# Another order of the three part products of every split float32 product, by tile, row pair and pass

## The chip, the cores and the metric

The kernel runs on one core of a Trainium2 chip. The metric is device time in microseconds (us) for one execution: 725.29 us before the change, the median of three runs from 724.9 to 725.68.

## The reference, cut to what matters

```python
g = sigmoid((x * gate_w).sum(-1, keepdims=True))          # x: 2048 x 576
q, k, v = split(x @ wqkv)                                 # 32 heads of 18
pq, pk = phi(q), phi(k)                                   # phi(t) = t+1 for t>0, else exp(t); + 1e-6
kv = einsum("bhsd,bhse->bhde", pk, v); z = pk.sum(s)      # linear attention
a = ((pq @ kv) / (pq . z + 1e-6)) @ wo
b = Cr @ (x @ Wr.T) - Ci @ (x @ Wi.T)                     # real part of a 2-D DFT; C: 2048 x 2048, W: 576 x 576
out = g * a + (1 - g) * b
```

## The kernel before, in words

TensorE multiplies here with operands rounded to a short float32 format. So each operand is held as two tiles, a high part (`hi_of`, an ACT copy into the short format, line 175) and a low part (`lo_of`, what is left over, a DVE subtraction, line 185), and each product of float32 matrices is made of **three part products** that add up in one PSUM bank: high by high (hh), high by low (hl) and low by high (lh). The first letter is the stationary operand, the second the moving one. A group of three is called a triple here. In `hh hl` and `hl hh` the two neighbours have the same stationary operand, in `hh lh` and `lh hh` the same moving one. Nearly all matmuls have a moving operand of 128 x 288 and a stationary one of 128 x 128.

The stages, in order of time, with the lines of their matmuls in the profile:

1. K (L532 for the first four row tiles, then L205, operands `wd` and `xs`): x times wk, 12 tiles of 28 matmuls, `steps` gives the order hh hl lh for each of four chunks of 128, and two matmuls for the rest.
2. x transposed times the features of k (L696, `pk` and `c`): per quarter four row tiles, three part products, two column halves that alternate (two banks); the order is `FULL`, hh hl lh. The small products with wv (L678, L681) follow.
3. Q (L205, `wd` and `xs`): as K, 16 tiles.
4. The attention output (L205, `mw` and `qs`): `m_steps`, 16 tiles, hh hl lh, `qs` being the transposed and normalised q. `transposed` makes the two `qs` tiles of a pair: TensorE transposes (L797), ACT makes the high parts, DVE the low parts. The low part is the last thing that a tile's first triple needs.
5. The hidden DFT (L979, `Hidden.product`): a 2x2 scheme with seven products in place of eight; for each of eight row tiles p seven products of two triples in the order `TURN` = hl hh lh and one matmul of 96 rows for the rest.
6. The sequence DFT (L1133, `sequence`): again seven products (the dictionary `PRODUCTS`, run in the order 1, 6, 2, 5, 7, 3, 4), eight row pairs j, each in four batches b of two inner tiles: a batch is 7 products x 2 tiles x 3 = 42 matmuls. Seven of the eight PSUM banks hold the seven sums of a row pair. Order `TURN`, and `FULL` in the very first batch. Behind the fourth batch of a row pair ACT and DVE read the banks in the order 1, 6 and 2, 7, 5, 7, 3, 4, combine them and store two row tiles.

Stages 5 and 6 run twice, for the real and the imaginary matrices. ACT and DVE make the high and low parts of the next batch of the matrix (`craw` to `c`) while TensorE multiplies. ACT, DVE and SP run in the order in which the code is written; TensorE does so from stage 4 on, and in stages 1 to 3 a scheduler sets its order.

Of the kernel before, what the change touches and what calls it, by code (L numbers as in the profile page):

```python
# [133 lines left out]
def kernel(  # L134
# [67 lines left out]
    def run(ps, pairs):  # L202
        pairs = list(pairs)
        for n, (a, b) in enumerate(pairs):
            nc.tensor.matmul(ps, a, b, start=(n == 0), stop=(n == len(pairs) - 1))  # L205

    def half(h):
        return slice(h * HALF, (h + 1) * HALF)
# [62 lines left out]

    def steps(xs, rhs):

        for c in range(KC):
            yield xs[:, c], rhs(c)
            yield xs[:, c], rhs(5 + c)
            yield xs[:, 5 + c], rhs(c)
        yield xs[:, 4], rhs(4)
        yield xs[:, 9], rhs(4)
# [407 lines left out]
    for c in range(5):  # L687
        ps = [bank(), bank()]
        passes = FULL if c < KC else FULL[:2]
        for q in range(NCU):  # L690
            t = xg_split.pop(0)
            for k in range(CU):
                s = q * CU + k
                for n, (a, b) in enumerate(passes):
                    for h in range(2):
                        nc.tensor.matmul(ps[h][:, :HALF], t[:, a, k], pk[s][:, b, half(h)],  # L696
                                         start=(s == 0 and n == 0),
                                         stop=(s == NT - 1 and n == len(passes) - 1))
            tick()
# [47 lines left out]
    def q_tile(i):  # L747
        xs = kept.pop(0) if i < KEPT else split.pop(0)
        for h in range(2):
            ps = bank()[:, :QH[h]]  # L750
            run(ps, steps(xs, lambda j: wqt.row(h, j)))
# [111 lines left out]

    def m_steps(qs, h):
        for c in range(KC):
            yield qs[:, c], mhi[:, c, half(h)]
            yield qs[:, c], mlo[:, c, half(h)]
            yield qs[:, 4 + c], mhi[:, c, half(h)]
        yield qs[:, 8], mhi[:, KC, half(h)]
        yield qs[:, 8], mlast[:, half(h)]  # L870
# [68 lines left out]
    class Hidden:  # L939
# [34 lines left out]
        def product(self, ps, p, k, start):  # L974
            x, (w, wl) = self.x[p, k], self.w[k]
            ops = [(x[:, a, c * P:c * P + P], w[:, 2 * c + b]) for c in range(2) for a, b in TURN]
            ops.append((self.rest[p][:96, 6 - k], wl[:96]))
# [113 lines left out]
    mix_ring = Ring(MIX_AT, D * 4, 4)  # L1091

    def sequence(m, g, src, dst, last=None, between=None):
        late, held, stores, rest_lows = [], [], [], []
        for n in range(NP * NB):
# [30 lines left out]
            if end and b == NB - 2:  # L1126
                continue
            for q, (l, f) in PRODUCTS.items():
                for b, c in held:
                    for k in range(BS):  # L1130
                        p = b * BS + k
                        for i, (x, y) in enumerate(TURN if n or b else FULL):
                            nc.tensor.matmul(ps[q], c[x][:, l, k], factors[p](y, f),  # L1133
                                             start=(p == 0 and i == 0),
                                             stop=(p == NP - 1 and i == 2))
            held.clear()
# [56 lines left out]
    for i in range(NT):  # L1193
# [162 lines left out]
```

## Time and profile before

| what | value |
|---|---|
| median of three runs | 725.29 us |
| the profiled execution's own time | 725.31 us |
| its span | 723.6 us |
| outside the span | 1.71 us |
| granted TensorE clock | 1.00 |
| matmuls and weight loads | 5436 each |
| of them L1133 / L205 / L979 / L696 | 2688 / 1266 / 784 / 448 |

PE in the profile's lines is the matmul, PEld the weight load that precedes each. A matmul's record lasts about 294 ns, though a new one begins every 132 ns, because records overlap in the pipeline. So the pace of a stage is read as the time from the first to the last start, divided by the number of matmuls less one, and not from the mean duration.

### The profile page before, as it was taken

How to read it: one execution, taken by the hardware profiler on the slowest of the kernel's cores; microseconds unless marked ns; L12 is line 12 of the kernel's file. 1: busy time of each engine (PE TensorE's matmuls, PEld its weight loads, DVE VectorE, ACT ScalarE, POOL GpSimd, SP SyncE). 2: the span in 40 equal slices, each digit the busy share in tenths (PEclk: the TensorE clock that was granted, in tenths of full speed). 3: DMA queues.
4: the chain of work that ended last, by engine and by line, in shares of the span. 5: the costliest groups of instructions: out<-in, count | busy, mean ns of one | idle time of the engine just before them, and what ended most of it. 6: DMA issues, size and time to landing. Idle time of an engine off the chain costs nothing.

```text
span 723.6 us, 13786 instructions
## 1 busy us (share of the span) xinstructions
PE 718.9 (99%) x5436; PEld 718.3 (99%) x5436; DVE 594.6 (82%) x954; ACT 331.8 (46%) x519; POOL 54.1 (7%) x94
## 2 busy tenths in 40 slices
PE   9999999999999999999999999999999999999998
PEld 9999999999999999999999999999999999999997
DVE  5699876787999828989999999857889988778884
ACT  5998445678644534453434334223535432342331
POOL 1112200050131100000010000000000000000000
PEclk9999999999999999999999999999999999999999
DMA  7388887874594699544475586889963543454440
GB/s 256 105 286 297 305 304 214 295 223 118 182 358 177 228 321 388 160 153 131 157 249 189 167 289 198 287 313 401 380 214 130 175 143 136 125 179 153 153 154 34
DMA packets 54836, 157.83 MB, mean 218 GB/s; under 512 B 6388, under 2 KB 12084, under 8 KB 53748
## 3 DMA queue, kind: packets, MB, share of 16 engines
q1 hardware_dynamic: 45716, 118.44, 48.5%
q0 software_dynamic: 8768, 38.12, 14.5%
q8 instruction: 43, 0.70, 0.4%
q10 hardware_dynamic: 288, 0.39, 0.2%
q14 instruction: 21, 0.17, 0.1%
HBM read 114.06 MB, written 41.39 MB: 215 GB/s over the span
## 4 chain that ended last, share of the span: by engine, by line
PE 93%; DVE 6%; issue 0%; ACT 0%; DVEq 0%; POOL 0%; POOLq 0%
PE bank L1133 49%; PE bank L205 18%; PE bank L979 14%; PE bank L696 8%; PE bank L532 2%; DVE qs L185 1%; DVE acc L775 1%; DVE pz L767 1%; DVE den L768 1%; PE bank L231 1%; PE bank L678 0%; DVE xb L185 0%; DVE den L772 0%; PE bank L797 0%; DVE xb L195 0%
## 5 line engine op out<-in xcount | busy, mean ns | idle before, releaser
L1133 PE MATMUL bank<-fh,c 128*128 128x288 f32 x1792 | 354.7, 294 | 0.0
L1133 PEld LDWEIGHTS bank<-fh,c 128*128 128x128 f32 x1792 | 286.7, 188 | 0.0
L1133 PE MATMUL bank<-fl,c 128*128 128x288 f32 x896 | 263.6, 294 | 0.0
L175 ACT ACTIVATE c<-craw 128x1792 fp32r<-128x1792 f32 (+1 forms) x84 | 121.3, 1447 | 169.9 <-DVE craw L195 161.2
L1133 PEld LDWEIGHTS bank<-fl,c 128*128 128x128 f32 x896 | 168.7, 188 | 0.0
L185 DVE TENSOR_TENSOR c<-craw,c 128x1792 fp32r<-128x1792 f32 (+4 forms) x86 | 141.9, 1653 | 1.5 <-ACT c L175 1.4
L195 DVE TENSOR_TENSOR craw<-craw 128x256 f32<-128x256 f32 (+1 forms) x192 | 97.9, 512 | 22.0 <-DMA craw<-in_ci_dram 13.6
L205 PE MATMUL bank<-wd,xs 128*128 128x288 f32 (+1 forms) x784 | 105.9, 295 | 0.0
L205 PEld LDWEIGHTS bank<-wd,xs 128*128 128x128 f32 x784 | 104.6, 188 | 0.0
L979 PE MATMUL bank<-wf,xf 128*128 128x288 f32 x588 | 91.1, 295 | 0.0
L979 PEld LDWEIGHTS bank<-wf,xf 128*128 128x128 f32 x588 | 83.4, 189 | 0.0
L205 PE MATMUL bank<-mw,qs 128*128 128x288 f32 x448 | 61.8, 296 | 0.1
L696 PE MATMUL bank<-pk,c 128*128 128x288 f32 x448 | 60.6, 296 | 0.0
L205 PEld LDWEIGHTS bank<-mw,qs 128*128 128x128 f32 x448 | 59.8, 188 | 0.5 <-DVE qs L185 0.4
L696 PEld LDWEIGHTS bank<-pk,c 128*128 128x128 f32 x448 | 59.7, 189 | 0.0
L370 DVE SCALAR_TENSOR_TENSOR acc<-bank,e 128x288 f32<-128x288 f32 x64 | 28.5, 452 | 17.3 <-ACT e L369 17.1
L195 DVE TENSOR_TENSOR ys<-bank,ys 128x288 f32<-128x288 f32 x63 | 28.8, 456 | 16.0 <-PE bank L1133 12.6
L185 DVE TENSOR_TENSOR fl<-fl,fh 128x864 fp32r<-128x864 f32 (+1 forms) x32 | 34.5, 1093 | 6.6 <-ACT fh L175 5.3
L175 ACT ACTIVATE fh<-fl 128x864 fp32r<-128x864 f32 (+1 forms) x32 | 29.8, 950 | 16.6 <-DVE fl L195 16.6
L195 DVE TENSOR_TENSOR fl<-bank,y 128x288 f32<-128x288 f32 x48 | 21.6, 450 | 15.8 <-PE bank L979 15.8
L979 PE MATMUL bank<-wf,xr 96*128 96x288 f32 x112 | 33.3, 298 | 0.0
L195 DVE TENSOR_TENSOR ys<-ys,bank 128x288 f32<-128x288 f32 x47 | 21.2, 450 | 12.4 <-PE bank L1133 11.8
(106 smaller groups left out, 639.6 us busy)
## 6 DMA issues: line engine op xcount, KB each, us to landing
xf<-xm SPq DMA_DIRECT2D x42, 512.0 KB, 8.4
craw<-in_cr_dram SPq DMA_DIRECT2D x32, 512.0 KB, 3.6
craw<-in_ci_dram SPq DMA_DIRECT2D x32, 512.0 KB, 3.7
xm<-xb POOLq DMA_DIRECT2D x8, 1024.0 KB, 5.8
wf<-wm SPq DMA_DIRECT2D x14, 576.0 KB, 6.2
xraw<-in_xa_dram SPq DMA_DIRECT2D x25, 320.0 KB, 3.5
xr<-xr SPq DMA_DIRECT2D x14, 448.0 KB, 8.0
xm<-xb POOLq DMA_DIRECT2D x8, 768.0 KB, 7.4
```

What stands on the lines that cost most here:

```text
L175: return nc.scalar.activation(dst, src, AF.Copy, bias=bias)
L185: nc.vector.tensor_tensor(out=dst, in0=src, in1=hi, op=ALU.subtract)
L195: nc.vector.tensor_tensor(out=dst, in0=a, in1=b, op=op)
L205: nc.tensor.matmul(ps, a, b, start=(n == 0), stop=(n == len(pairs) - 1))
L231: nc.tensor.matmul(warm[:, :P], ones_f, ones_f, start=True, stop=True)
L370: nc.vector.scalar_tensor_tensor(dst, ps, 0.0, e, op0=ALU.max, op1=ALU.add)
L532: nc.tensor.matmul(ps[i][h], x[:, i_x * P:(i_x + 1) * P], wkt.row(h, j), start=(c == 0 and n == 0), stop=(c == KC and n == 1))
L696: nc.tensor.matmul(ps[h][:, :HALF], t[:, a, k], pk[s][:, b, half(h)], start=(s == 0 and n == 0), stop=(s == NT - 1 and n == len(passes) - 1))
L767: nc.vector.scalar_tensor_tensor(pz, acc[2 * k + i], EPS, zb, op0=ALU.add, op1=ALU.mult)
L768: nc.vector.tensor_reduce(out=d[:, i], in_=pz.rearrange("p (h d) -> p h d", d=DH), op=ALU.add, axis=AX.X)
L979: nc.tensor.matmul(ps, a, b, start=(start and n == 0), stop=(n == len(ops) - 1), skip_group_check=True)
L1133: nc.tensor.matmul(ps[q], c[x][:, l, k], factors[p](y, f), start=(p == 0 and i == 0), stop=(p == NP - 1 and i == 2))
```

## The change

The order inside the triples, and in places the order of halves, inner tiles and products, now varies:

- `TURNS` lists the six orders of a triple: 0 `hl hh lh`, 1 `lh hh hl`, 2 `hh hl lh`, 3 `hh lh hl`, 4 `lh hl hh`, 5 `hl lh hh`. K, Q and the attention output take order i % 6 for row tile i, the hidden DFT p % 6 for row tile p, stage 2 the order (4c + q) % 6 for chunk c and quarter q; in six of its quarters all of the first half come ahead of the second.
- The sequence DFT keeps its order in the first batch of a sequence and in the last batch of each row pair. In the other batches the first sequence takes order j % 6 for row pairs 0 to 5 and mixtures of orders 0 and 1 for 6 and 7; the second takes order 0 or 1 or both by product, with the inner tiles interleaved for j = 0, the products in the order 1, 2, 6, 5, 3, 7, 4 for j = 1 and 2, and in reversed order for j = 5 and 6.

No matmul is added or taken away, and none has other operands.

```diff
+    TURNS = "hl hh lh", "lh hh hl", "hh hl lh", "hh lh hl", "lh hl hh", "hl lh hh"
+    def orders(turn):
+        return [tuple("hl".index(c) for c in part) for part in turn.split()]
...
-    def steps(xs, rhs):
+    def steps(xs, rhs, turn="hh hl lh"):
         for c in range(KC):
-            yield xs[:, c], rhs(c)
-            yield xs[:, c], rhs(5 + c)
-            yield xs[:, 5 + c], rhs(c)
+            for a, b in orders(turn):
+                yield xs[:, 5 * a + c], rhs(5 * b + c)
...
-        run(ps, steps(xs, lambda j: wkt.row(h, j)))
+        run(ps, steps(xs, lambda j: wkt.row(h, j), TURNS[i % 6]))
...
-            for k in range(CU):
-                s = q * CU + k
-                for n, (a, b) in enumerate(passes):
-                    for h in range(2):
+            turn = passes if c == KC else orders(TURNS[(c * NCU + q) % 6])
+            parts = [(k, n, h) for k in range(CU) for n in range(len(turn)) for h in range(2)]
+            if 6 <= c * NCU + q < 12:
+                parts.sort(key=lambda part: part[2])
+            for k, n, h in parts:
...
-        ops = [... for c in range(2) for a, b in TURN]
+        ops = [... for c in range(2) for a, b in orders(TURNS[p % 6])]
...
+    def variant(j, second):
+        A, B = (orders(turn) for turn in TURNS[:2])
+        first, by = list(PRODUCTS), False
+        mixed = 1, 2, 6, 5, 3, 7, 4
+        if not second:
+            t = orders(TURNS[j % 6])
+            turned = ([t, t], [t, t]) if j < 6 else ([(A, B), (B, A)][j - 6],) * 2
+        else:
+            turned = [[t, t] for t in ((A, A), (A, A), (B, B), (B, A), (A, B), (A, A), (B, B),
+                                       (A, A))[j]]
+            by = j == 0
+            if j in (1, 2):
+                first = mixed
+            if j in (5, 6):
+                first = first[::-1]
+        return first, turned, by
...
-            for q, (l, f) in PRODUCTS.items():
+            turned = [TURN, TURN], [TURN, TURN]
+            first, by = list(PRODUCTS), False
+            if n == 0:
+                turned = [FULL, FULL], [FULL, FULL]
+            elif b < NB - 1:
+                first, turned, by = variant(j, last is not None)
+            for q in first:
+                l, f = PRODUCTS[q]
                 for b, c in held:
-                    for k in range(BS):
-                        p = b * BS + k
-                        for i, (x, y) in enumerate(TURN if n or b else FULL):
+                    parts = [(k, i) for k in range(BS) for i in range(3)]
+                    if by:
+                        parts.sort(key=lambda part: part[1])
+                    for k, i in parts:
+                        p, (x, y) = b * BS + k, turned[f % 2][k][i]
...
-            run(ps[:, :HALF], m_steps(qs, h))
+            run(ps[:, :HALF], m_steps(qs, h, TURNS[i % 6]))
```

`m_steps` is changed as `steps` is, and the Q tiles take the order i % 6 as the K tiles do.

**Place 1**: TensorE in the attention output, the first half of row tile i = 10 (order 4 now). `mw_222` is the high and `mw_223` the low part of the matrix, `qs_364` holds both parts of q; the rows are in the program's order, a wait stands at the matmul that it holds up. Before:

```order
L205 MATMUL bank_3196<-mw_222_1735,qs_364_3128 128x288 [waits Activation_49]
L205 MATMUL bank_3196<-mw_223_1736,qs_364_3128 128x288
L205 MATMUL bank_3196<-mw_222_1735,qs_364_3128 128x288 [waits DVE_49]
L205 MATMUL bank_3196<-mw_222_1735,qs_364_3128 128x288
L205 MATMUL bank_3196<-mw_223_1736,qs_364_3128 128x288
```

With the change:

```order
L205 MATMUL bank_3196<-mw_222_1735,qs_364_3128 128x288 [waits DVE_49]
L205 MATMUL bank_3196<-mw_223_1736,qs_364_3128 128x288 [waits Activation_49]
L205 MATMUL bank_3196<-mw_222_1735,qs_364_3128 128x288 x2
L205 MATMUL bank_3196<-mw_223_1736,qs_364_3128 128x288
L205 MATMUL bank_3196<-mw_222_1735,qs_364_3128 128x288 x2
```

The matmul that waits for DVE's low part has moved from the third place to the first, ahead of the two that need the high part alone.

**Place 2**: TensorE in the first sequence DFT, row pair j = 1, first batch (order 1 now). `c_507` is the high and `c_508` the low part of the matrix (stationary), `fh` and `fl` those of the factor (moving). Before:

```order
L1133 MATMUL bank_4389<-fl_414_3508,c_507_4279 128x288 [waits Activation_49]
L1133 MATMUL bank_4389<-fh_412_3506,c_507_4279 128x288
L1133 MATMUL bank_4389<-fh_412_3506,c_508_4280 128x288 [waits DMAHW6_49,DVE_49]
L1133 MATMUL bank_4389<-fl_423_3584,c_507_4279 128x288
L1133 MATMUL bank_4389<-fh_421_3582,c_507_4279 128x288
L1133 MATMUL bank_4389<-fh_421_3582,c_508_4280 128x288
```

With the change:

```order
L1164 MATMUL bank_4389<-fh_412_3506,c_508_4280 128x288 [waits DMAHW6_49,DVE_49]
L1164 MATMUL bank_4389<-fh_412_3506,c_507_4279 128x288 [waits Activation_49]
L1164 MATMUL bank_4389<-fl_414_3508,c_507_4279 128x288
L1164 MATMUL bank_4389<-fh_421_3582,c_508_4280 128x288
L1164 MATMUL bank_4389<-fh_421_3582,c_507_4279 128x288
L1164 MATMUL bank_4389<-fl_423_3584,c_507_4279 128x288
```

The triple runs backwards: the low part of the matrix is wanted two matmuls earlier, and neighbours still share one operand.

**Place 3**: TensorE in the second sequence DFT, row pair j = 5, first batch, from its first matmul on (products reversed now). `bank_7871` is the sum of product 1, `bank_7872` of product 6, `bank_7876` of product 3 and `bank_7877` of product 4; these names are the program's, which physical bank stands behind one is settled when it is first written. Before:

```order
L1133 MATMUL bank_7871<-fl_656_6083,c_807_7760 128x288 [waits Activation_49]
L1133 MATMUL bank_7871<-fh_654_6081,c_807_7760 128x288
L1133 MATMUL bank_7871<-fh_654_6081,c_808_7761 128x288 [waits DMAHW2_49,DVE_49]
L1133 MATMUL bank_7871<-fl_665_6159,c_807_7760 128x288
L1133 MATMUL bank_7871<-fh_663_6157,c_807_7760 128x288
L1133 MATMUL bank_7871<-fh_663_6157,c_808_7761 128x288
L1133 MATMUL bank_7872<-fl_658_6085,c_807_7760 128x288 [waits Activation_49]
```

With the change:

```order
L1164 MATMUL bank_7877<-fl_658_6085,c_807_7760 128x288 [waits Activation_49]
L1164 MATMUL bank_7877<-fh_654_6081,c_807_7760 128x288
L1164 MATMUL bank_7877<-fh_654_6081,c_808_7761 128x288 [waits DMAHW2_49,DVE_49]
L1164 MATMUL bank_7877<-fl_667_6161,c_807_7760 128x288
L1164 MATMUL bank_7877<-fh_663_6157,c_807_7760 128x288
L1164 MATMUL bank_7877<-fh_663_6157,c_808_7761 128x288
L1164 MATMUL bank_7876<-fl_656_6083,c_807_7760 128x288 [waits Activation_49]
```

Product 4 stands where product 1 stood, and product 3 where product 6 stood; the waits stay at their places in the row.

More of the change, by code (lines that the diff above doesn't have):

```diff
@@ L691 @@
             t = xg_split.pop(0)
-            for k in range(CU):
-                s = q * CU + k
-                for n, (a, b) in enumerate(passes):
-                    for h in range(2):
-                        nc.tensor.matmul(ps[h][:, :HALF], t[:, a, k], pk[s][:, b, half(h)],
-                                         start=(s == 0 and n == 0),
-                                         stop=(s == NT - 1 and n == len(passes) - 1))
+            turn = passes if c == KC else orders(TURNS[(c * NCU + q) % 6])
[3 more added lines that the diff above has]
+            for k, n, h in parts:
+                s, (a, b) = q * CU + k, turn[n]
+                nc.tensor.matmul(ps[h][:, :HALF], t[:, a, k], pk[s][:, b, half(h)],
+                                 start=(s == 0 and n == 0),
+                                 stop=(s == NT - 1 and n == len(turn) - 1))
             tick()
@@ L750, in q_tile @@
             ps = bank()[:, :QH[h]]
-            run(ps, steps(xs, lambda j: wqt.row(h, j)))
+            run(ps, steps(xs, lambda j: wqt.row(h, j), TURNS[i % 6]))
             g = gate[:, TURNED[i]:TURNED[i] + 1]
@@ L862, in split_m, with m_steps @@
         lo_of(mlast[:, half(h)], mrest[:, half(h)], mhi[:, KC, half(h)])
-    def m_steps(qs, h):
+    def m_steps(qs, h, turn):
         for c in range(KC):
-            yield qs[:, c], mhi[:, c, half(h)]
-            yield qs[:, c], mlo[:, c, half(h)]
-            yield qs[:, 4 + c], mhi[:, c, half(h)]
+            for a, b in orders(turn):
+                yield qs[:, 4 * a + c], (mlo if b else mhi)[:, c, half(h)]
         yield qs[:, 8], mhi[:, KC, half(h)]
@@ L975, in product @@
             x, (w, wl) = self.x[p, k], self.w[k]
-            ops = [(x[:, a, c * P:c * P + P], w[:, 2 * c + b]) for c in range(2) for a, b in TURN]
+            ops = [(x[:, a, c * P:c * P + P], w[:, 2 * c + b]) for c in range(2) for a, b in orders(TURNS[p % 6])]
             ops.append((self.rest[p][:96, 6 - k], wl[:96]))
```

6 lines of the change are left out of this document (3 added, 3 removed).

## The prediction

> **What bounds the kernel now.** The page comes first: busy time by engine, the 40 slices and the chain that ended last.
>
> ```profile
> span 723.6 us, 13786 instructions
> ...
> PE 718.9 (99%) x5436; PEld 718.3 (99%) x5436; DVE 594.6 (82%) x954; ACT 331.8 (46%) x519; POOL 54.1 (7%) x94
> ...
> PE   9999999999999999999999999999999999999998
> ...
> PEclk9999999999999999999999999999999999999999
> ...
> PE 93%; DVE 6%; issue 0%; ACT 0%; DVEq 0%; POOL 0%; POOLq 0%
> ```
>
> TensorE is busy in every slice at the full granted clock. DVE at 82% is no rival to it. Next, the waits of the weight loads, where TensorE's own waits appear:
>
> ```profile
> PEld bank L231 <- POOL ones_f L224: 1.1, 1, 1.1
> PEld bank L205 <- DVE qs L185: 0.4, 1, 0.4
> ```
>
> There is one wait at the start and one of 0.4 us in the attention output. So the time is the number of matmuls times their pace, and since the change adds no matmul, only two things can move it: a new wait, or another **pace**. The third view is the pace by stage. In rows of the timeline (start, duration, count) it is the duration less one record of 0.29 us, by the count less one:
>
> ```profile
> 20.26 44.75 PE L205 MATMUL bank<-wd,xs 128*128 128x288 f32 x336
> 64.85 19.34 PE L696 MATMUL bank<-pk,c 128*128 128x288 f32 x144
> 124.95 4.32 PE L696 MATMUL bank<-pk,c 128*128 128x288 f32 x32
> ```
>
> K (hh hl lh, neighbours share at most the stationary operand) runs at 44.46/335 = 132.7 ns, stage 2 at 19.05/143 = 133.2 and its last chunk, which has hh and hl alone, at 4.03/31 = 130.0. In the sequence DFT a window from one batch's first start to the next one's gives the pace of its 42 matmuls (first number the width in us):
>
> ```profile
> 324.66:330.19 5.53, 5.53 (x44) 5.53 (x43) 5.47 (x6) 1.31 (x2) 0.00 (x0) 1.00 0.27 98
> 330.19:335.72 5.53, 5.53 (x44) 5.53 (x43) 4.96 (x8) 3.59 (x3) 0.00 (x0) 1.00 0.32 95
> 313.49:319.08 5.59, 5.59 (x44) 5.59 (x43) 5.41 (x10) 1.85 (x2) 0.00 (x0) 1.00 1.00 381
> 319.08:324.66 5.58, 5.58 (x45) 5.58 (x43) 5.21 (x6) 5.58 (x5) 0.00 (x0) 1.00 0.10 41
> 548.34:553.91 5.57, 5.57 (x44) 5.57 (x43) 5.21 (x6) 5.57 (x5) 0.00 (x0) 1.00 0.00 1
> ```
>
> From the third batch on it is 5.53 us, 131.7 ns each, with very different work on DVE, ACT and the DMA engines beside it. The first batch (hh hl lh) takes 5.59, but the second has the order hl hh lh that all later ones have, and takes 5.58 and 5.57 in the two sequences. So the pace of 131.7 is not the order's alone; the spread between all these rows, 130.0 to 133.2 ns, is what an order can be worth at most by this trace.
>
> **The change part by part.** The sum is made against the profiled execution's own 725.31 us, 0.02 us above the median.
>
> *Waits, attention output.* In row tile 10 the order lh hl hh puts the matmul that waits for DVE's low part first (place 1). The rows around it:
>
> ```profile
> 236.55 1.60 DVE L185 TENSOR_TENSOR qs<-bank,qs 128x512 fp32r<-128x512 f32 x3
> 237.29 3.47 PEld L205 LDWEIGHTS bank<-mw,qs 128*128 128x128 f32 x26 [0.36 <-DVE qs L185]
> ...
> 216.13 7.67 PE L205 MATMUL bank<-mw,qs 128*128 128x288 f32 x56
> 232.95 8.05 PE L205 MATMUL bank<-mw,qs 128*128 128x288 f32 x56
> 241.73 7.83 PE L205 MATMUL bank<-mw,qs 128*128 128x288 f32 x56
> ```
>
> Two matmuls that now fill part of the wait come behind it: 2 x 0.13 = 0.26 us later, for them and all behind them in the queue. But the pair that holds tile 12 took 7.83 us where an undisturbed pair takes 7.67; these 0.16 us are also a wait for DVE, tile 12's order is as harmless as before (hl hh lh), and DVE does not wait for TensorE there. A later TensorE waits less. I take 0.26 - 0.16 = **+0.10**, with +0.26 as the upper end and 0.10 as the lower.
>
> *Waits elsewhere.* Low parts are wanted up to two matmuls, 0.27 us, earlier in orders 1 and 4. The two closest places:
>
> ```profile
> 41.66 0.81 DVE L185 TENSOR_TENSOR xs<-xraw,xs 128x640 fp32r<-128x640 f32 x1
> 339.19 2.02 DVE L185 TENSOR_TENSOR c<-craw,c 128x1792 fp32r<-128x1792 f32 x1
> 341.26 0.29 PE L1133 MATMUL bank<-fl,c 128*128 128x288 f32 x1
> ```
>
> K tile 10 begins 168 matmuls behind 20.26, at 42.56; its low part is done at 42.47. In the sequence, row pair 1, the second batch begins at 341.26 and its low part is done at 341.21; now the first matmul wants it, not the third. Both are in time, by 0.09 and 0.05 us. Behind that wait would stand the whole batch, and the batch's end is what the next work of DVE on the banks waits for. I cost both at nothing; without this cover they cost 0.1 to 0.3 us together.
>
> *Pace, stages 1 to 5.* The rows offer one price. In hl hh lh (131.7) one neighbour pair shares the moving operand, in hh hl lh (132.7) none: 1.0 ns a matmul, 3 ns a triple. Orders 0, 1, 3 and 5 have such a pair, 2 and 4 have none. Triples that gain it: K 64 of 96, Q 88 and the output 88 of 128 each, stage 2 some 32. Triples that lose it: 56 in the hidden DFT (p = 2 and 4, two passes x 7 products x 2), 84 in the first sequence (j = 2 and 4, three batches x 14), 28 in the second (j = 0). Net 104 x 3 ns = **-0.3 us**. The ends: if all 1680 matmuls of K, Q, output and stage 2, five in six of them turned, came down to 131.7, 1400 x 1.0 = -1.4; if they went up to stage 2's 133.2, +0.7.
>
> *Pace, sequences.* 41 batches change their order (first sequence 7 row pairs x 3, second 6 x 3 and two of j = 0); the other 23 keep theirs. Between 5.53 and 5.58 us, that is 0 to 41 x 0.05 = +2.1 us. Most rows hold the even pace whatever stands beside them, so I take a quarter, **+0.5**.
>
> Sum: 725.31 + 0.10 - 0.3 + 0.5 = **725.6 us**, no change by the measure used here: 0.2%, 1.45 us, is about what a measurement of this kernel can tell from none.
>
> **The rivals.**
>
> *A. The sequences lose their even pace* (slower). All 41 batches run as the second one did: +2.1 in place of +0.5, 727.2 us. For it: two batches of the very same instructions and order ran 1% slower at each sequence's beginning, so the even pace is a state that can be missed. Against it: 60 of 64 batches have it. It decides from 0.04 us a batch on.
>
> *B. Sharing is worth more than I take* (faster). The turned 1400 matmuls of the first five stages come to the 130.0 ns of stage 2's last chunk: 1400 x 2.7 = -3.8, 721.6 us. Against it: that chunk is 4 us short, and in stage 2 proper, with as much sharing of the stationary operand between halves, the pace is the worst of all.
>
> *C. The reversed products wait for their banks* (slower). Product 4 runs first in row pairs 5 and 6 of the second sequence, and if it took the bank that product 3 of the row pair before had, it would wait for DVE's reading of it:
>
> ```profile
> 653.52 0.29 PE L1133 MATMUL bank<-fl,c 128*128 128x288 f32 x1
> 653.67 0.46 DVE L195 TENSOR_TENSOR ys<-bank,ys 128x288 f32<-128x288 f32 x1
> ```
>
> The row pair begins at 653.52, the bank is read until 654.13, and waking takes 0.05 (low part done at 237.24, load at 237.29): 0.66 us twice, 726.9 us. Against it stands place 3: the first product in the row waits as the first did before, the second as the second, so the banks go by the order of first use and the free one comes first.
>
> *D. A broken run of one stationary operand costs its load* (slower). Sharing of the stationary operand falls by some 350 pairs (112 in K, Q and output, 56, 112, and some 70 in stage 2). By the nearest row, 130.0 against 133.2, that is 350 x 3.2 ns = +1.1, 726.7 us, at the edge of slower; with a whole load it would be tens of us. Against it: the page has as many loads as matmuls, 5436 each, so nothing is spared today. The Trainium skill, "TensorE: Matmul & The Clock Gate", Part 2, says that weights typically stay put across many matmuls, so that one loads once and multiplies repeatedly; by that rule this change would be a loss, and the trace, with a load for every matmul, disagrees.
>
> **How the numbers follow.** Forecast 0.56, A 0.27, B 0.12, C 0.03, D 0.02. Slower by over 0.2% (above 726.74) is A, C and D, 0.32; faster B, 0.12; within 0.2% the forecast, 0.56. The forecast's own range is 725.31 + 0.10 - 1.4 = 724.0 to 725.31 + 0.26 + 0.3 + 0.7, about 726.6. With A, whose worst case adds 2.1 to 725.31 + 0.26 + 0.3 = 728.0, the range is 724.0 to 728.0; B is left out.
>
> **What would show it.** The wait at tile 10 should grow from 0.36 to about 0.6 us and the pair of tile 12 shorten to 7.67. The batches of the sequences should stay at 5.53 us; 5.57 or more in those with orders 2 to 5 means A. K, Q and output should come down by some 0.5 ns a matmul; three times that means B. No wait should appear at the start of row pairs 5 and 6 (C). The prediction is wrong if the pace depends on the order by more than the 130.0 to 133.2 ns seen, or if a wait appears in a stage that has none.

## The result, and the profile after

The median of five runs is 727.74 us (727.19 to 727.8) against 725.18 us (724.9 to 725.68) of the kernel before on the same chip. The ratio is 1.0034, 95% interval 1.0023 to 1.0045: slower by 2.56 us, with an interval of some 1.7 to 3.3. The time lies in the stated range, but only because that takes in rival A's worst case: the forecast's own range ended at about 726.6. The likeliest case, no change, did not come.

The page of the kernel after, as that of before: span and busy time, and the chain that ended last.

```profile
span 725.4 us, 13787 instructions
...
PE 720.9 (99%) x5436; PEld 720.4 (99%) x5436; DVE 595.4 (82%) x954; ACT 332.0 (46%) x519; POOL 54.2 (7%) x94
...
PE 99%; DVE 0%; DVEq 0%; issue 0%; POOL 0%; POOLq 0%
```

TensorE has the same 5436 matmuls and 2.0 us more to do on them. All the other engines do what they did. The waits of the weight loads:

```profile
PEld bank L236 <- POOL ones_f L229: 1.1, 1, 1.1
PEld bank L205 <- DVE qs L185: 0.2, 1, 0.2
```

No wait came; one became shorter. So the loss is **pace**. The two sequences as one window each, from their first matmul to the next stage's, or to the last matmul of all (width in us first, then busy time and instructions by engine). Before:

```profile
313.49:490.66 177.17, 177.17 (x1347) 177.17 (x1345) 155.68 (x215) 64.37 (x46) 6.42 (x9) 1.00 0.65 220
542.73:719.78 177.05, 177.05 (x1345) 177.05 (x1344) 146.52 (x202) 59.07 (x43) 0.00 (x0) 1.00 0.42 138
```

After:

```profile
313.33:491.39 178.06, 178.06 (x1346) 178.06 (x1345) 155.64 (x215) 64.44 (x46) 6.42 (x9) 1.00 0.65 220
543.55:721.64 178.09, 178.09 (x1346) 178.09 (x1344) 146.76 (x202) 58.89 (x43) 0.00 (x0) 1.00 0.42 138
```

They grew by 0.89 and 1.04 us. By windows of the same kind the hidden DFT ahead of each grew by 0.30 (51.97 to 52.27) and 0.09 (52.07 to 52.16). K changed by +0.04, stage 2 by -0.07, Q with its transposes by +0.14, the attention output by -0.28 (from the start of the last Q tile, which it overlaps), and the start-up (L532 before, L536 now) by -0.3. The last is no effect: over the other runs here the start-up differs from that of before by -0.7 to +0.2 us, in kernels that leave it as it was. The two profiled executions differ by 727.19 - 725.31 = 1.88 us, and the stages' sum is the same within rounding. The one of after was the fastest of its five, so the medians stand further apart.

Some batches of 42 matmuls in the kernel after: the first, second and fourth of row pair 1 in the first sequence (order 1, and the fourth in order 0 again), the first and fourth of row pair 4 (order 4, then 0), and the fourth of row pair 1 in the second sequence (as before, behind three with mixed products).

```profile
335.57:341.17 5.60, 5.60 (x44) 5.60 (x43) 5.36 (x10) 1.71 (x1) 0.00 (x0) 1.00 0.58 199
341.17:346.75 5.58, 5.58 (x45) 5.58 (x43) 5.48 (x9) 1.71 (x1) 0.00 (x0) 1.00 0.58 203
...
352.30:357.87 5.57, 5.57 (x44) 5.57 (x43) 4.47 (x7) 2.00 (x2) 0.00 (x0) 1.00 0.31 94
402.38:407.92 5.54, 5.54 (x44) 5.54 (x43) 5.37 (x9) 1.71 (x1) 0.00 (x0) 1.00 0.62 201
418.99:424.60 5.61, 5.61 (x45) 5.61 (x43) 4.46 (x7) 2.00 (x2) 1.23 (x2) 1.00 0.80 295
...
582.63:588.25 5.62, 5.62 (x44) 5.62 (x43) 4.47 (x7) 2.00 (x2) 0.00 (x0) 1.00 0.27 93
```

All of these took 5.53 before. The batches that did not change pay too: the fourth ones behind orders 1 to 4 or mixed products take 5.56 to 5.62 us. Over both sequences the 41 changed batches lost 1.16 us and the unchanged ones 0.77. The row pairs of the first sequence with one other order, in ns, start to start:

| order in batches 1 to 3 | 1st | 2nd | 3rd | 4th (order 0) |
|---|---|---|---|---|
| j = 5: order 5, hl lh hh | 5533 | 5534 | 5533 | 5533 |
| j = 1: order 1, lh hh hl | 5604 | 5577 | 5554 | 5572 |
| j = 3: order 3, hh lh hl | 5606 | 5556 | 5553 | 5573 |
| j = 2: order 2, hh hl lh | 5540 | 5534 | 5533 | 5612 |
| j = 4: order 4, lh hl hh | 5540 | 5533 | 5533 | 5613 |

Order 0 itself takes 5533 where no other order comes before it. So the six orders act in three classes: 0 with 5, 1 with 3, 2 with 4. Sharing does not make these classes: orders 0, 1, 3 and 5 have a shared moving operand, 2 and 4 have none. What does is the place of the one part product with a low moving operand (hl): first in 0 and 5, last in 1 and 3, in the middle in 2 and 4.

### The profile page after: what moved, and what is told of

It is laid out like the page before. It is cut to its first block, busy times and chain, and to the rows that moved or that the text cites. A ratio compares the mean times of both kernels' runs of the same rounds, so it can differ in the third digit from the quotient of the medians.

```text
span 725.4 us, 13787 instructions
## 1 busy us (share of the span) xinstructions
PE 720.9 (99%) x5436; PEld 720.4 (99%) x5436; DVE 595.4 (82%) x954; ACT 332.0 (46%) x519; POOL 54.2 (7%) x94
## 4 chain that ended last, share of the span: by engine, by line
PE 99%; DVE 0%; DVEq 0%; issue 0%; POOL 0%; POOLq 0%
PE bank L1164 49%; PE bank L205 23%; PE bank L984 14%; PE bank L702 8%; PE bank L536 2%; PE bank L803 1%; PE bank L236 1%; PE bank L682 0%; DVE row L1180 0%; DVE ys L195 0%; PE bank L685 0%; PE bank L804 0%; DVEq L1383 0%; POOL ones_f L229 0%; DVEq L1180 0%
## 5 line engine op out<-in xcount | busy, mean ns | idle before, releaser
L1164 PE MATMUL bank<-fh,c 128*128 128x288 f32 x1792 | 349.7, 295 | 0.0
L1164 PEld LDWEIGHTS bank<-fh,c 128*128 128x128 f32 x1792 | 283.8, 188 | 0.0
L1164 PE MATMUL bank<-fl,c 128*128 128x288 f32 x896 | 253.3, 295 | 0.0
L1164 PEld LDWEIGHTS bank<-fl,c 128*128 128x128 f32 x896 | 164.9, 188 | 0.0
L185 DVE TENSOR_TENSOR c<-craw,c 128x1792 fp32r<-128x1792 f32 (+4 forms) x86 | 141.9, 1653 | 2.1 <-ACT c L175 2.0
L185 DVE TENSOR_TENSOR fl<-fl,fh 128x864 fp32r<-128x864 f32 (+1 forms) x32 | 34.5, 1093 | 6.6 <-ACT fh L175 5.4
```

The lines of the kernel that those rows point to most:

```text
L185: nc.vector.tensor_tensor(out=dst, in0=src, in1=hi, op=ALU.subtract)
L1164: nc.tensor.matmul(ps[q], c[x][:, l, k], factors[p](y, f), start=(p == 0 and i == 0), stop=(p == NP - 1 and i == 2))
```

## The experiments

A run's time without an interval beside it is that of one execution; there the argument rests on the trace.

**Where it sits.** The first two kernels are the two halves of the change: one keeps the new orders in the sequences alone, the other everywhere else.

```diff
-        run(ps, steps(xs, lambda j: wkt.row(h, j), TURNS[i % 6]))
+        run(ps, steps(xs, lambda j: wkt.row(h, j)))
...
-        ops = [... for c in range(2) for a, b in orders(TURNS[p % 6])]
+        ops = [... for c in range(2) for a, b in TURN]
```

> Only the orders of the two sequence DFTs change; K, stage 2, Q, attention output and hidden DFT keep the orders of before. Theory 1 (the loss sits in the sequences, whose batches leave the pace of 5.53 us): the changed kernel's trace has +0.9 and +1.0 us in the two sequences, so this one is 1.9 us over before, about 727.1 us, with the same batches slow. Rival (the loss is made of the other stages and of how the program starts): within 0.4 us of before, 725.2 to 725.6.

```diff
-            elif b < NB - 1:
-                first, turned, by = variant(j, last is not None)
```

> The change without the sequences: these keep the order of before in every batch, all other stages have the new orders. Theory 1: only the hidden DFT's +0.3 to +0.4 us and the attention output's changed wait are left, 725.3 to 725.9 us, and all batches of the sequences from the third on take 5.53 us. Rival (the loss sits in the other stages): 726.7 to 727.7 us.

The sequences alone: 726.86 us, ratio 1.0023 (1.0015 to 1.0032). The rest alone: 725.08, ratio 0.9999 (0.999 to 1.0008). In the first of the two the sequences take

```profile
313.08:491.19 178.11, 178.11 (x1346) 178.10 (x1345) 155.74 (x215) 64.34 (x46) 6.42 (x9) 1.00 0.64 219
543.27:721.36 178.09, 178.09 (x1346) 178.09 (x1344) 146.77 (x202) 58.92 (x43) 0.00 (x0) 1.00 0.41 137
```

0.94 and 1.04 us more than before, as in the kernel after, and in the second every batch after the first two of a sequence takes 5.53 again, but for one of 5.64 that begins with a gap of 25 ns. So the loss sits in the sequences. In the second kernel the hidden DFT lost its 0.3 and 0.1 and the attention output gained its 0.29, as in the kernel after, and they cancel. The two differences, +1.53 and -0.25, make 1.3, while the whole made 2.56; with intervals of some 0.6 to 0.8 each side these can just agree. That the two halves add up to the whole is read from the windows of the stages, not from the medians.

**Which orders.** In the next kernel the first sequence has hl lh hh in its first three batches, all products as before, and the second has the triples of before, with the products in the mixed order.

```diff
+                if last is None:
+                    turned = [[orders(TURNS[5])] * 2] * 2
+                else:
+                    first = 1, 2, 6, 5, 3, 7, 4
```

> All stages as before but for the sequences. First sequence: order 5 (hl lh hh) in the first three batches of each row pair, hl hh lh in the fourth. Second sequence: the triples of before (hl hh lh), but the products in the order 1, 2, 6, 5, 3, 7, 4 in the first three batches. Theory 2 (the pace follows the sequence of moving operands, and orders with the low moving operand in the same place are alike): the first sequence stays at 5.53 us in every batch from the third on, although no two neighbours share a stationary operand any more. Theory 3 (sharing of an operand, or any switch of order, sets the pace): its batches take 5.55 us or more. Second sequence: theory 2 with the starts of the moving operands (they alternate between 0 and 128 bytes of 256 from product to product in this order, in blocks of odd and even products in the order of before) gives 5.58 to 5.62 us in every batch, +1.5 us in all; if only the order within a triple counts, 5.53.

It took 727.06 us. The first sequence's batches (first row) stay at 5.53 (but for one of 5.57) although hl lh hh separates the two products that share a stationary operand. The second sequence's row pair 1 (other rows) shows the loss with triples that nobody touched:

```profile
335.91:341.44 5.53, 5.53 (x44) 5.53 (x43) 5.29 (x10) 1.71 (x1) 0.00 (x0) 1.00 0.59 202
...
565.31:570.86 5.55, 5.55 (x44) 5.55 (x43) 5.32 (x9) 1.71 (x1) 0.00 (x0) 1.00 0.59 201
...
576.45:582.04 5.59, 5.59 (x45) 5.59 (x43) 3.77 (x6) 1.71 (x1) 0.00 (x0) 1.00 0.30 97
582.04:587.66 5.62, 5.62 (x45) 5.62 (x44) 4.42 (x7) 2.00 (x2) 0.00 (x0) 1.00 0.29 93
```

The sequence grew by 1.57 us. An order of products, which changes nothing inside a triple, costs more here than the changed orders of triples and products did together (1.04).

Then one order all through a sequence but for its first batch, so that nothing is switched: lh hh hl in the first, hh hl lh in the second.

```diff
+            else:
+                turned = [[orders(TURNS[1 if last is None else 2])] * 2] * 2
```

> All stages as before but for the sequences, where one order holds in every batch but the very first: lh hh hl in the first sequence, hh hl lh in the second, with no switch back in the fourth batch. Theory 4 (a switch disturbs a settled state, each order settles to about the same pace): after two batches the first sequence settles at 5.53 to 5.55 us and the second at 5.53, the two sequences together at most 0.7 us longer than before. Rival (an order has a pace of its own): lh hh hl stays at 5.57 to 5.60 us, the first sequence 1.2 to 2.2 us longer.

It took 726.69 us. One batch of each sequence:

```profile
401.85:407.40 5.55, 5.55 (x44) 5.55 (x43) 5.38 (x9) 1.71 (x1) 0.00 (x0) 1.00 0.59 201
...
565.13:570.71 5.58, 5.58 (x45) 5.58 (x44) 5.34 (x9) 1.71 (x1) 0.00 (x0) 1.00 0.58 200
```

The sequences settle at 5553 and 5580 ns a batch (+0.68 and +1.38 us), but for one of 5644 in the first, at the close place of row pair 1 that the prediction names, where the loads have a gap of some 30 ns. This fitted neither expectation: the loss is not the switching alone, and not one price per order either, since hh hl lh takes 5580 here and 5533 in the kernel after, where it follows batches of hl hh lh.

**What the orders change: starts.** One more thing differs between orders of the same operands: the row of addresses. The start of an operand is the address in the on-chip memory where its part of each partition begins; what counts below is this address modulo 256 bytes. A product q of `PRODUCTS` reads chunk f of the factor as its moving operand. The factor's high part is seven chunks of 288 floats, 1152 bytes or 4.5 times 256, and its low part lies behind in the same way. So the high chunks start at 128, 0, 128, ... modulo 256 bytes for f = 0, 1, 2, ..., the low ones the other way round, and every stationary tile of the sequences starts at 128. For even f the start of the moving operand is that of the stationary one in hh and lh and not in hl, for odd f the reverse. With e for equal and d for different, orders 0 and 5 read d e e, 1 and 3 e e d, 2 and 4 e d e: the three classes. The products' f in the order of before are 0, 4, 1, 3, 5, 2, 6: the row turns over twice in a batch; in the mixed order (0, 1, 4, 3, 2, 5, 6) it does so at nearly every product. This is the theory of starts, theory 5 in the expectations.

A small kernel measures it by itself. It leaves the reference's work out: 17 runs of 168 matmuls of 128x128 by 128x288, one line of code each, no waits after the loads.

```python
for d in go(triples(O[0], False, (128, 128))):
    nc.tensor.matmul(*mm(d), start=d["start"], stop=d["stop"], skip_group_check=True)
```

The arguments are the order (0), a moving operand of its own for each matmul (`False`), and the starts of high and low moving operands; the stationary ones start at 128 (`st`), in the last two lines at 0 (`su`).

> Not the reference's work: 17 runs of 168 matmuls of the kernel's size (stationary 128 x 128, moving 128 x 288, seven banks in turn, six matmuls to a bank, no waits between), each run with its own source line, over the same data; only the order within triples and the start of the moving operand in SBUF, counted in bytes modulo 256, differ. The pace of a run is its last start less its first by 167. Theory 5 (the pace hangs on the starts of the moving operands): all starts at 0 give 133.3 ns, as the second half of the attention output in the kernel before, all at 128 give 131.7, as its first half; with all starts alike the three orders hl hh lh, lh hh hl and hh hl lh give one pace; with high parts at 128 and low parts at 0, exchanged in the odd products, hl hh lh gives 131.7, lh hh hl 132.2 and hh hl lh 132.9 as the settled batches of the kernels did, and exchanged from product to product 133 or more. Rival (the order of high and low or the sharing of an operand counts by itself): the starts change nothing, and the orders differ among themselves at equal starts too.

Rows of its timeline (start, duration, line, count). L67 has all moving starts at 128, L69 at 64; L85 and L89 have all at 128 and orders 0 and 2 with moving operands that neighbours share (L87, order 1, has the same 22.28); L95 has a stationary start of 0 with moving starts of 0, L97 with 128:

```profile
34.85 22.28 PE L67 MATMUL bank<-mv,st 128*128 128x288 f32 x168
56.97 22.56 PE L69 MATMUL bank<-mv,st 128*128 128x288 f32 x168
...
234.95 22.28 PE L85 MATMUL bank<-mv,st 128*128 128x288 f32 x168
...
279.19 22.28 PE L89 MATMUL bank<-mv,st 128*128 128x288 f32 x168
...
346.07 22.28 PE L95 MATMUL bank<-mv,su 128*128 128x288 f32 x168
368.19 22.56 PE L97 MATMUL bank<-mv,su 128*128 128x288 f32 x168
```

Read as the prediction reads such rows, (22.28 - 0.29) / 167 = 131.7 ns and (22.56 - 0.29) / 167 = 133.4 ns (133.3 from start to start). Where all starts are equal these three orders do not differ, nor does it matter whether neighbours share a moving operand. In the sequences' own row of starts, 42 matmuls at a time (first batch of a run, then its third): L75 has order 2 after order 0, L91 order 2 after a run with equal starts.

```profile
123.76:129.33 5.57, 5.57 (x44) 5.57 (x43) 0.00 (x0) 0.00 (x0) 1.00 0.01 3
134.87:140.41 5.54, 5.54 (x45) 5.54 (x44) 0.00 (x0) 0.00 (x0) 1.00 0.00 0
...
301.31:306.92 5.61, 5.61 (x44) 5.61 (x43) 0.00 (x0) 0.00 (x0) 1.00 0.00 0
312.50:318.08 5.58, 5.58 (x44) 5.58 (x43) 0.00 (x0) 0.00 (x0) 1.00 0.00 0
```

Same order, same starts, and it settles at 5533 or at 5580 ns from start to start by what came before, the two values that order 2 has in the kernel after and in the run with one order throughout. With mixed starts the pace of these runs lies between 131.7 and 133.3 ns, in a pattern that depends on the row of starts and on its history. Most switches of order cost some 40 to 85 ns in the next batch and up to 46 in the one behind it; those to orders 2 and 4 in the table cost only 7. The 5533, 5553, 5580 and 5587 ns seen in the sequences are 131.74, 132.2, 132.86 and 133.0 ns a matmul.

A first test of it in the kernel, the first sequence with products of even f ahead of those of odd f (4, 1, 3, 6, 5, 7, 2), the second with another order in each row pair's second batch alone:

```diff
+                if last is None:
+                    first = 4, 1, 3, 6, 5, 7, 2
+                elif b % 2:
+                    turned = [[orders(TURNS[4])] * 2] * 2
```

> All stages as before but for the sequences. First sequence: triples as before, products in the order 4, 1, 3, 6, 5, 7, 2 in the first three batches of each row pair, which keeps even and odd moving tiles in two blocks. Theory 5 (starts of the moving operands): 5.53 us a batch, at most 5.55. Rival (any other order of products costs): 5.55 to 5.62 as with 1, 2, 6, 5, 3, 7, 4. Second sequence: order lh hl hh in the second batch of each row pair alone, hl hh lh in the others. Theory 4 (a state that a switch disturbs and that decays): the second batch takes 5.54 us and the third, which has the order of before, 5.61, +0.08 us for each row pair and 0.7 in all. Rival (each order has its own pace): only the second batch differs, the third takes 5.53.

It took 726.53 us beside 725.78 of before. The first row is a batch of the first sequence, the others are the second and third of row pair 1 in the second:

```profile
407.73:413.26 5.53, 5.53 (x44) 5.53 (x43) 5.46 (x7) 1.71 (x1) 0.00 (x0) 1.00 0.66 204
...
571.09:576.67 5.58, 5.58 (x44) 5.58 (x43) 5.46 (x8) 1.71 (x1) 0.00 (x0) 1.00 0.64 197
576.67:582.29 5.62, 5.62 (x45) 5.62 (x44) 3.68 (x5) 1.71 (x1) 0.00 (x0) 1.00 0.30 99
```

Another order of products that keeps blocks of one start costs nothing in the pace. One batch of the first sequence takes 5994 ns: its third load waits 0.44 us for DVE's low part. This is the 0.46 us by which that sequence grew; why DVE was late there alone is not shown. One batch in another order costs 0.09 us a row pair, half of it in the batch behind: 5575 and 5579 ns in most row pairs, 5582 and 5613 in this one.

**Taking the starts away.** These two are the decisive ones. The matmuls, banks, dependencies and orders stay, but each moving operand of the sequences is read 32 floats off where that is needed to bring its start to 128 (with the orders of after) or to 0 (with those of before, and 0 for 1 in the condition). Their products are so made of shifted rows.

```diff
+        def moving(self, y, f):
+            k, t = (f % 4, self.parts[f // 4][1]) if y else (f, self.hi)
+            o = k * HALF
+            if (f + y) % 2 == 1:
+                o += 32 if k == 0 else -32
+            return t.rearrange("p f n -> p (f n)")[:, o:o + HALF]
```

> The kernel after, with all its orders, but in both sequences every moving operand is read 128 bytes off where that is needed for it to start at 128 modulo 256 bytes, as every stationary one does (so those products are made of shifted rows; the same matmuls, banks, waits and orders). Theory 5 (pace goes by the start of the moving operand against the stationary one's, and the orders cost only because they change the row of starts): all 64 batches take 42 x 131.7 = 5.53 us, the sequences fall by 0.9 + 1.0 us to about 177.0 and 176.9, the median to about 725.7, the same as before. Rival (the orders cost as such: operands that neighbours share, banks, or changing the order at a batch): the batches stay at 5.54 to 5.63 us as in the kernel after and the median at 727.6.

> The kernel before, with its orders, but in both sequences every moving operand is read 128 bytes off where that is needed for it to start at 0 modulo 256 bytes, while the stationary ones start at 128 (products of shifted rows). Theory 5: all 64 batches take 42 x 133.3 = 5.60 us, 0.067 more than before, in all 62 x 0.067 + 2 x 0.02 = +4.2 us, 729.4 us. Rival (starts do not matter with these operands): 5.53 us a batch, 725.2 us.

With equal starts the orders of after cost nothing: 725.06 us, ratio 1.0 (0.9991 to 1.0009). Its sequences:

```profile
313.03:490.19 177.16, 177.16 (x1346) 176.99 (x1345) 155.54 (x215) 64.43 (x46) 6.41 (x9) 1.00 0.63 219
542.36:719.19 176.83, 176.83 (x1346) 176.83 (x1344) 146.56 (x202) 58.86 (x43) 0.00 (x0) 1.00 0.42 138
```

They lie 0.90 and 1.26 us under those of after. Only two batches stand out, 5627 and 5633 ns in row pair 1 of the first sequence, and not by the pace of their orders: the load at their border waits, `PEld bank L1171 <- DVE c L185: 0.2, 1, 0.2` in the waits. This is the edge of 0.05 us that the prediction costed at nothing; TensorE came a little earlier here, and the low part was not there.

With all starts apart the orders of before cost 728.84 us, ratio 1.005 (1.0034 to 1.0065). One batch:

```profile
408.29:413.89 5.60, 5.60 (x45) 5.60 (x43) 5.53 (x7) 1.71 (x1) 0.00 (x0) 1.00 0.67 202
```

All 64 take 5.60; the sequences grew by 2.04 and 2.01 us, and no order was touched. So the sequences' loss is shown to come through the starts, and not through the order as such.

**What could be won, and where the rule ends.** In stage 2 and the attention output the second column half starts at 0. Cut at 320 columns in place of 288, both halves start at 128:

```diff
+    def cut(h):
+        return slice(320 * h, 320 + 256 * h)
```

> The kernel before, with all its orders, but the columns of stage 2 and of the attention output are cut 320 and 256 instead of 288 and 288. Both moving operands then start at 128 modulo 256 bytes, as the stationary ones do; with the even cut the second half starts at 0. Theory 5 (a matmul starts every 131.7 ns where the moving operand's start equals the stationary one's modulo 256 bytes, and every 133.3 ns where not): stage 2 loses about 416 x 1.5 ns = 0.6 us and the attention output 224 x 1.6 ns = 0.36 us, the median falls by about 1.0 us, to 0.9986 of before, and the mean pace of a pair of 320 and 256 columns is 131.7 ns. Rival (the start matters only in the small test, or a wider cut costs what it gains): no change, 0.9995 to 1.0005, with stage 2 still at 133.2 ns.

Beside it a grid of starts, 19 runs in a small kernel as above, the reference's work left out again:

> A small kernel that leaves the reference's work out: 19 runs of 168 matmuls, each with operands of its own, order of a triple the same throughout, no waits. Stationary start at 128 modulo 256 bytes, moving at 128, 32, 64, 96, 160, 192, 224, 0; stationary at 0, moving at 64, 192, 0; stationary at 64, moving at 0, 64, 128, 192; then stationary at 128 with 320 and 256 columns, moving at 128 and at 0. Theory 5 as stated: 131.7 ns only where the two starts are equal modulo 256, 133.3 ns elsewhere (so 131.7 in the 1st, 11th and 13th run alone). Rival 5b (the moving operand's start decides in steps: both starts in the same half of 256 bytes, or both a multiple of 128): 131.7 ns in more of them, at 160, 192 and 224 with a stationary start of 128 above all. Last four: 320 columns at 131.7 + 32 / 2.4 = 145.0 ns and 256 at 118.4 ns with equal starts, and 1.6 ns more with different ones.

The cut gained nothing: 725.14 us, ratio 0.9999 (0.999 to 1.0008), stage 2 at 133.2 as before. The grid says why. L76 has moving 192 against a stationary start of 128, L78 224, L82 64 against 0; L96 and L98 have 320 and 256 columns with equal starts, L100 and L102 with starts 128 apart:

```profile
125.75 22.38 PE L76 MATMUL bank<-mv,st 128*128 128x288 f32 x168
147.97 22.29 PE L78 MATMUL bank<-mv,st 128*128 128x288 f32 x168
...
192.49 22.28 PE L82 MATMUL bank<-mv,su 128*128 128x288 f32 x168
...
348.26 24.80 PE L96 MATMUL bank<-mv,st 128*128 128x320 f32 x168
372.90 20.32 PE L98 MATMUL bank<-mv,st 128*128 128x256 f32 x168
393.05 24.80 PE L100 MATMUL bank<-mv,st 128*128 128x320 f32 x168
417.69 20.10 PE L102 MATMUL bank<-mv,st 128*128 128x256 f32 x168
```

From start to start 320 columns take 146.7 ns in both cases, and 256 take 120.0 with equal starts and 118.7 with different ones. A pair of 320 and 256 with equal starts averages 133.3, which is what the even cut had at its worst. So the theory fell in its general form. With 288 columns a distance of 0, 64 or 96 bytes between the moving and the stationary start, modulo 256, gave 131.7 to 132.2 ns, and 32, 128, 160, 192 or 224 gave 133.3; with other widths it is another rule. In the sequences only 0 and 128 occur, and there it holds.

Last, the kernel before with 288 columns, and the moving starts brought to 128 by shifted reads in stage 2, the attention output and the hidden DFT (for its matmuls of full height), so that their products are of shifted rows or columns:

```diff
+    def near(h):
+        return slice(256 * h, 256 * h + HALF)
```

> The kernel before, with its orders, but in stage 2, the attention output and the hidden DFT every full moving operand is read 128 bytes off where that is needed for it to start at 128 modulo 256 bytes, as the stationary ones do, still 288 columns wide (products of shifted columns or rows). Theory 5: stage 2 loses 416 x 1.5 ns = 0.6 us, the attention output 224 x 1.6 ns = 0.36 us, the hidden DFT comes from 132.5 to 131.7 ns a matmul, 784 x 0.8 ns = 0.6 us; the median falls by about 1.6 us to 723.6, ratio 0.9978. Rival, from the run with columns cut 320 and 256, which gained nothing (starts matter in the sequences alone): no change, 725.2 us.

724.38 us, ratio 0.9991 (0.9982 to 0.9999): a third of what was expected. Stage 2 gave its 0.56 in all, but its last chunk, hh and hl alone, got slower: 4.37 us for 32 matmuls, 131.6 ns each, where the prediction's row has 4.32 and 130.0.

```profile
123.63 4.37 PE L699 MATMUL bank<-pk,c 128*128 128x288 f32 x32
```

With starts of 128 and 0 by turns this chunk ran faster than any run of 288 columns with equal starts. So equal starts are not the best pace everywhere; what sets 130.0 there is open.

In the attention output each second half went from 1734 or 1740 to 1711 ns for 13 starts, some 0.4 us in all, but the waits for DVE's low parts grew:

```profile
PEld bank L205 <- DVE qs L185: 0.8, 2, 0.6
```

0.8 us in place of 0.4, so that 0.11 was left. The hidden DFT did not move (+0.07 and -0.03). Its full matmuls came from 132.2 and 132.5 to 132.0 ns, but the step behind the matmul of 96 rows that ends each product grew from 134.8 to some 137.6 ns on average; why is open. A kernel that has these starts and the right operands needs other addresses for several tiles; it was not tried, and 0.1% is what it would be worth.

## Why the prediction was right and wrong

*What bounds it, and that only waits or pace can move it*: right. The waits fell by 0.2 us in all, and the rest is pace.

*Wait at tile 10 (+0.10)*: wrong, it shrank. Rows of the kernel after, the pair of tiles that holds tile 10, its wait, the pair that holds tile 12, and DVE's low parts for tile 10:

```profile
232.81 7.89 PE L205 MATMUL bank<-mw,qs 128*128 128x288 f32 x56
...
236.71 3.75 PEld L205 LDWEIGHTS bank<-mw,qs 128*128 128x128 f32 x28 [0.18 <-DVE qs L185]
...
241.44 7.67 PE L205 MATMUL bank<-mw,qs 128*128 128x288 f32 x56
```

```profile
235.97 1.61 DVE L185 TENSOR_TENSOR qs<-bank,qs 128x512 fp32r<-128x512 f32 x3
```

Before, DVE began 236.55 - 232.95 = 3.60 us after the pair, now 235.97 - 232.81 = 3.16, 0.44 sooner. The two matmuls that came behind the wait cost what they were to cost: 0.36 + 0.26 - 0.44 = 0.18, the wait in the row. The pair of tile 12 shortened to 7.67, as was said. The step that failed is "DVE does not wait for TensorE there": it is true at that place, but 48 us earlier DVE had waited for ACT, and ACT for TensorE. In the last Q tiles the scheduler that orders TensorE until stage 4 puts the nine transposes 24 matmuls later with the change. Before:

```profile
183.29 0.82 PE L797 MATMUL bank<-ident,acc 128*128 128x128 f32 x6
...
183.97 6.23 PE L205 MATMUL bank<-wd,xs 128*128 128x288 f32 x45
...
187.47 0.17 ACT L754 ACTIVATE gate<-bank 128x1 f32<-128x1 f32 x1 [0.43 <-PE bank L205]
```

After:

```profile
182.76 3.52 PE L205 MATMUL bank<-wd,xs 128*128 128x288 f32 x25
...
186.12 1.04 PE L803 MATMUL bank<-ident,acc 128*128 128x128 f32 x8
...
186.72 0.15 ACT L760 ACTIVATE gate<-bank 128x1 f32<-128x1 f32 x1
```

ACT's wait of 0.43 us is gone, and with it DVE's wait for ACT behind it (0.66 at 188.46). DVE's queue runs some 0.6 us earlier, 0.44 of which is left at tile 10. In the five runs that leave the orders and operands of Q and the output as before, DVE begins 3.58 to 3.60 us after the pair; in the three with the changed orders there 3.14 to 3.16. Which order made the scheduler turn is not tested.

*Two close places costed at nothing*: right here (no wait in K, 0.03 us in the sequence), and the second was as thin as it was said to be, as the run with equal starts showed.

*Pace, stages 1 to 5 (-0.3)*: wrong in its price. 1.0 ns for a shared moving operand was read from two rows that differed in their starts as well; with equal starts orders with and without sharing take the same 131.7 ns. K stayed (+0.04 where -0.2 was to come by 64 x 3 ns). The hidden DFT, forecast at +0.17 by 56 x 3 ns, took 0.39 more; it does so as well where the sequences keep their orders (the second kernel), and whether the starts are the cause there was not tested. With the shorter waits of the output left out, the five stages grew by some 0.5 us. The sum also took off 112 triples of the sequences, which the next term holds already; without them it is 216 x 3 ns = -0.65.

*Pace, sequences (+0.5)*: this is the term that decided, and it was mis-sized: +1.93 was measured. The quarter rested on "most rows hold the even pace whatever stands beside them". They did, but all those rows have one order; they could say nothing of another. The rows that could, the second batches with 5.58 and 5.57, were quoted as rival A's evidence, and they were what a switch of order costs. Two things were also not seen: that unchanged batches would pay (+0.03 to +0.09 for most of the fourth ones, 0.77 in all), and that some changed ones (orders 5, 2, 4, reversed products) would pay next to nothing, so that the 41 changed batches lost 1.16, 0.03 each on average. That the total came near the bound of 41 x 0.05 = +2.1 is luck: two errors that nearly cancel.

*Rivals*. A was right in stage and sign. Its 727.2 came near by luck, as said, and its sign, 5.57 or more in batches of orders 2 to 5, failed: orders 2, 4 and 5 take 5.53 or 5.54, and the batches that lose time have orders 1 and 3 or mixtures, or follow another order. It called the even pace a state that can be missed, which fits, but knew nothing of the starts. B fell: the 130.0 ns of the short chunk was no price of sharing, since the chunk has 131.6 with equal starts and the same sharing. C fell as argued: there is no wait at row pairs 5 and 6, and the former, which differs from before by its reversed products alone, takes 5533 ns a batch. D fell: the loads are 5436 as before, and in the run with equal starts the batches of orders 3 and 5, which share no stationary operand within a triple, take the same 5.53 us as those of orders 2 and 4, which do.

*The sign of being wrong*: by its own words the prediction is wrong if the pace leaves 130.0 to 133.2 ns. Single batches of 5612 to 5620 ns did, with 133.6 to 133.8 ns a matmul; the first batch of the second sequence had 5.61 us before the change, too.

## What to carry to other kernels

A bound read from rows that all have the same order is no evidence for another order: if the rows that differ take longer, give them the weight. Where nothing waits and the number of matmuls is fixed, look at the addresses: list the start of the moving and of the stationary operand of each matmul, and try matmuls with the same distance together. Then measure: one stretch here was faster with its starts by turns. And a reordering under a scheduler moves more than the diff shows: compare the whole order of the engine, as the transposes here.

## What the runs showed of the hardware that was not expected

- With a weight load for each matmul of 128x128 by 128x288, a new one begins every 131.7 ns (132.2 in two rows) or every 133.3 ns by the distance of the two operands' starts modulo 256 bytes, where this is the same for all (1.2%).
- A column costs (146.7 - 120.0) / 64 = 0.417 ns. At that price 133.3 ns is the time of 320 columns, 32 more than the matmul has, and 146.7 and 120.0 are those of 352 and 288, also 32 more than theirs. The better pace is 1.6 ns under that with 288 columns, 1.3 ns with 256, and did not show with 320 at the two distances tried.
- With mixed distances the pace settles in one of several patterns (131.74, 132.2, 132.86, 133.0 ns), and the same order can settle in two of them, by what ran before. One stretch of 32 matmuls with two distances by turns ran at 130.0 ns, under the 131.6 that it has with equal ones. What sets this is open.
